# An attention kernel's row maxima: turned on VectorE and spread through DRAM, in place of a turn on TensorE

## The chip, the cores and the metric

The kernel runs on one core of a Trainium2 chip. The metric is the device time of one execution in microseconds (us). Before the change the median of three runs is 1738.05 us (1737.16 to 1738.56). Engines: TensorE (PE; its weight loads are listed as PEld), VectorE (DVE), ScalarE (ACT), GpSimd (POOL) and SyncE (SP), which here only issues transfers.

## The reference

Four layers, A B A B, each a residual branch on x of 2048 tokens by 640 channels, 32 heads of 20 channels, in float32:

```
x = x + A(layernorm(x));  x = x + B(layernorm(x));  x = x + A(layernorm(x));  x = x + B(layernorm(x))

A: linear attention over all tokens, with phi(t) = (t > 0 ? t + 1 : exp(t)) + 1e-6
B: the tokens in 4 segments of 512; in segment s, for each head:
   p     = softmax(q k^T * 20^-0.5 + mask)        # causal inside the segment
   a_dot = p v
   a_mem = phi(q) M / (phi(q) z + 1e-6)           # memory of the segments before s
   o     = sigmoid(beta) * a_mem + (1 - sigmoid(beta)) * a_dot
   M += phi(k)^T v;  z += sum phi(k)
```

The change is in B's softmax. To exponentiate safely, each row of logits (one query of one head) needs its maximum taken off.

## The kernel before, in words

Two streams of work are woven by a small planner in `run` (L1307): `dense` (L1226), which has the projections, layer A, the memories and the output products, and `attend` (L1302), which has the softmax attention of the B layers. Each step yields a cost, and the stream with the lower total goes next; attention yields a fixed `SLOT` after each stretch. PE's instructions keep the order in which the program issues them (`MANUAL`). On the other engines and on SP's queue a list scheduler sets the order: an instruction that it holds ready may go ahead of an earlier one that it holds not ready. `issue_after` puts instructions behind a given one of the same engine.

`attention` (L1104) works on groups of four heads: 8 groups in each of 4 segments in each of 2 B layers, so 64 groups. Each turn of its loop is a **slot** of three **stretches** (L55 to L58), and each entry names an operation and which group it is for: 0 the new one, 1 the one before, 2 the one before that. The dense stream's work comes in between the stretches. So a group goes through three slots:

- `stacks` (L985) loads the group's queries and keys, split into two f16 parts and laid out as 60 rows a head (3 products of 20 channels), from DRAM into `qs` and `ks`: two heads in one half of the partitions (parity 0, rows 0 to 59) and two in the other (parity 1, rows 64 to 123). That is four issues on SP's queue (L993). `qs` and three fixed `ks` rotate, three of each. The entry "load" does this a slot ahead, and puts the issues behind the row transfers issued last (`self.rowed`).
- `row_max` (L998): PE forms the logits of a block of queries against the keys up to it (L1007), and DVE adds the mask and takes the row maximum in one pass (L1013). Five such steps a slot, MAXES 0 to 4, fill `mg`: a 128-partition tile with one value per parity, head and block of 128 queries, 16 columns.
- `split_max` (L1017), at the end of the third stretch: DVE turns the 16 maxima of a query into two f16 parts, negated and scaled (L1022, L1023), in `m2`: 128 x 32.
- `max_rows` (L1027), the entry "rows" in the first stretch of the next slot, after the first group of weighted sums ("sum", 0): PE transposes `m2` with an f16 identity into a PSUM bank (L1031), ACT copies the 32 x 128 result to `mt` (L1033), and two transfers on SP's queue put it into rows 60, 61, 124 and 125 of `qs` (L1036). `ks` holds a constant in the same rows, so the product over 62 rows has the maximum taken off.
- `scores` (L1039): PE's product over 62 rows, keys against queries (L1048), ACT's exp (L1052), POOL's causal mask on the diagonal blocks (L1059). EXPS 0 and 1 come in the second stretch of that same slot, 2 and 3 in the third, 4 at the start of the slot after. EXPS 0 is the first reader of rows 60 and 61 (parity 0), then of 124 and 125 (parity 1).
- `weigh` (L1067) has PE multiply the exponentials with the values, four heads side by side in 32 columns each (L1075), `evacuate` (L1079) copies the sums out (ACT, L1081), and `normalize` (L1083) turns them and divides (L1088 to L1099).

PSUM's eight banks go round for all of this. SP's queue also carries the projections' stores of split queries and keys (`nat` to `qd` and `kd`, L859 to L863), loads of x (L330) and loads of phi(q) (L762, L770). The projections' weights are fetched on POOL's queue (L275).

## Time and profile before

| what | us |
|---|---|
| three runs, median (lowest, highest) | 1738.05 (1737.16, 1738.56) |
| the profiled execution, its own time | 1736.07 |
| its span, first to last instruction | 1734.4 |
| granted TensorE clock, mean | 0.998 of full |
| PE busy | 1666.1 |
| transpose on PE (L1031), 64 times | 14.0 |
| copy on ACT (L1033), 64 times | 16.7 |
| issues of the row transfers (L1036), 128 of 4.0 KB | 0.617 each (median) |

The profile is one execution. "Busy" is the time in which an engine works on an instruction; matmuls are pipelined and overlap, so the sum of their lengths is more than the time that they fill. A group's row gives its line in the kernel, engine, operation, output and inputs by their names, shape and count, then busy time and mean length, then how long the engine stood idle ahead of these instructions and what it waited for (`<-`). In rows of the timeline the first number is the start in us from the span's start, the second the length. A name ending in q (SPq) is an engine's queue of issues: the length of a row there is that of the issue, not of the transfer. The chain of work that ended last is followed back from the last instruction, each step to what released it.

### The profile page before, as it was taken

Reading aid. Unit: us, or ns where it says so; the run is one execution under the profiler, and the core shown is the slowest. Engines: PE = TensorE matmul, PEld = TensorE weight load, DVE = VectorE, ACT = ScalarE, POOL = GpSimd, SP = SyncE. Lnnn points to the kernel's source line nnn. Section 1 sums busy time; section 2 is a strip of 40 time slices with the busy share of each in tenths; the row PEclk is TensorE's granted clock in tenths of the full one; section 3 lists DMA queues with packets and bytes.
Section 4 is the critical chain, followed back from the end, with each engine's and each line's share of the span. In section 5 each row is a group of like instructions: output and inputs, shape, how many; then the busy total and the mean of one; then the engine's idle time right before and its main releaser. Section 6 shows DMA issues by size and latency. Waiting matters only on the chain.

```text
span 1734.4 us, 36014 instructions
## 1 busy us (share of the span) xinstructions
PE 1666.1 (96%) x13032; PEld 1047.5 (60%) x13032; DVE 1180.9 (68%) x3849; ACT 969.7 (56%) x1818; POOL 517.7 (30%) x982
## 2 busy tenths in 40 slices
PE   6999999999999999999999999999999999999998
PEld 4676667664565576556556777666546545645555
DVE  8645534577787677759864456746777877878773
ACT  5545433357557645667675544333665576666673
POOL 1543350012123312334351301221422432233452
PEclk9999999999999999999999999999999999999999
DMA  7522452422322322352211303423232323223432
GB/s 262 184 109 95 150 195 97 139 76 82 113 71 73 113 96 68 120 179 95 78 48 51 103 32 122 175 98 116 75 102 85 112 81 108 93 82 111 131 115 92
DMA packets 118330, 187.58 MB, mean 108 GB/s; under 512 B 13949, under 2 KB 79613, under 8 KB 115849
## 3 DMA queue, kind: packets, MB, share of 16 engines
q1 hardware_dynamic: 105896, 142.68, 25.5%
q0 software_dynamic: 3040, 21.63, 3.4%
q10 hardware_dynamic: 9216, 20.98, 3.1%
q8 instruction: 103, 1.69, 0.4%
q14 instruction: 75, 0.61, 0.1%
HBM read 106.05 MB, written 78.64 MB: 106 GB/s over the span
## 4 chain that ended last, share of the span: by engine, by line
PE 78%; DVE 10%; ACT 6%; issue 2%; POOL 2%; DMA 1%; SPq 1%; ACTq 0%; POOLq 0%; DVEq 0%
PE ps L395 32%; PE ps L381 17%; PE ps L1075 7%; PE ps L1048 4%; ACT pe L1052 3%; PE ps L1007 3%; PE ps L319 3%; PE ps L564 3%; PE ps L450 3%; DVE ps L1013 2%; PE ps L1088 1%; PE ps L891 1%; PE ps L730 1%; DVE st L338 1%; DVE xn L479 1%
## 5 line engine op out<-in xcount | busy, mean ns | idle before, releaser
L1013 DVE CUSTOM_DVE_ANT_0 ps<-ps,maskw 128x512 f32<-128x512 f32 (+3 forms) x1024 | 472.5, 519 | 38.0 <-PE ps L1007 35.7
L1052 ACT ACTIVATE pe<-ps,lsc 128x512 f32<-128x512 f32 x640 | 394.8, 696 | 87.6 <-PE ps L1048 84.9
L1059 POOL TENSOR_SCALAR_AFFINE_SELECT pe<-pe 128x256 f32<-128x256 f32 (+1 forms) x640 | 229.7, 365 | 449.2 <-ACT pe L1052 444.0
L395 PEld LDWEIGHTS <-xT 128*128 128x128 f16 x2880 | 280.3, 98 | 114.6 <-issue 9.3
L395 PEld LDWEIGHTS <-oT 128*128 128x128 f16 x1920 | 185.7, 98 | 80.5 <-issue 7.0
L1075 PE MATMUL ps<-pe,v 128*32 128x512 f32 (+3 forms) x2048 | 162.2, 436 | 11.5 <-POOL pe L1059 5.1
L395 PE MATMUL ps<-w_Bo,oT 128*128 128x320 f16 x960 | 142.3, 302 | 2.8 <-ACT pe L1052 1.1
L1013 DVE DVE_READ_ACCUMULATOR2_ANT mg<- 128x1 f32 x1024 | 143.9, 141 | 0.0
L381 PE MATMUL ps<-xT,w_Bq 128*128 128x512 f16 x600 | 140.2, 380 | 1.9 <-ACT pe L1052 0.8
L395 PE MATMUL ps<-w_Bv,xT 128*128 128x320 f16 x960 | 139.7, 300 | 0.8 <-DVE otok L1095 0.6
L381 PE MATMUL ps<-xT,w_Bk 128*128 128x512 f16 x600 | 138.8, 380 | 1.2 <-ACT pe L1052 1.2
L395 PE MATMUL ps<-w_Ak,xT 128*128 128x320 f16 x960 | 136.1, 300 | 0.0
L1007 PE MATMUL ps<-ks,qs 60*128 60x512 f16 (+3 forms) x1024 | 123.1, 298 | 6.7 <-ACT pe L1052 2.9
L856 DVE SCALAR_TENSOR_TENSOR nat<-ps,nat 128x512 f16<-128x512 f32 x80 | 55.2, 690 | 89.2 <-ACT nat L855 89.1
L1048 PE MATMUL ps<-qs,ks 62*128 62x512 f16 (+3 forms) x1024 | 105.9, 301 | 3.0 <-DMA qs<-mt 1.5
L1075 PEld LDWEIGHTS ps<-pe,v 128*32 128x32 f32 x2048 | 65.3, 109 | 71.9 <-issue 45.8
L421 POOL TENSOR_SCALAR e<-e 128x320 f32<-128x320 f32 (+1 forms) x52 | 82.9, 1594 | 82.4 <-ACT e L417 78.2
L855 ACT ACTIVATE nat<-ps 128x512 f16<-128x512 f32 x80 | 48.2, 603 | 91.8 <-PE ps L381 69.2
L381 PEld LDWEIGHTS <-w_Bk 128*128 128x128 f16 x600 | 57.3, 98 | 65.5 <-issue 5.6
L381 PEld LDWEIGHTS <-w_Bq 128*128 128x128 f16 x600 | 56.7, 98 | 65.9 <-issue 7.8
L1007 PEld LDWEIGHTS <-qs 60*128 60x128 f16 x1024 | 50.0, 94 | 70.9 <-issue 44.7
L343 POOL TENSOR_TENSOR rs<-rs,mhalf 128x1 f32<-128x1 f32 x48 | 27.0, 563 | 218.8 <-DVE rs L342 218.7
(217 smaller groups left out, 2630.7 us busy)
## 6 DMA issues: line engine op xcount, KB each, us to landing
x<-xn ACTq DMA_DIRECT2D x48, 320.0 KB
qs<-qd SPq DMA_DIRECT2D x128, 120.0 KB
ks<-kd SPq DMA_DIRECT2D x128, 120.0 KB
xo<-x SPq DMA_DIRECT2D x48, 320.0 KB
pqi<-pqd SPq DMA_DIRECT2D x32, 320.0 KB
qd<-nat SPq DMA_DIRECT2D x40, 256.0 KB
kd<-nat SPq DMA_DIRECT2D x40, 256.0 KB
x<-in_A_x SPq DMA_DIRECT2D x16, 320.0 KB
```

What stands on the lines that cost most here:

```text
L319: nc.tensor.transpose(pt[:, (c - c0) * P:(c - c0 + 1) * P], src[:, c * P:(c + 1) * P], self.ident)
L381: nc.tensor.matmul(p, w[:, c, a, t * P:(t + 1) * P], xT[:, c, b, :], start=k == 0, stop=k == 3 * C - 1)
L395: nc.tensor.matmul(p, xT[:, c, a, i * P:(i + 1) * P], w[:, c, b, n * HN:(n + 1) * HN], start=k == 0, stop=k == 3 * C - 1)
L421: nc.gpsimd.tensor_scalar(e, e, 1.0, eps, op0=OP.min, op1=OP.add)
L450: nc.tensor.matmul(nd[:, lo - k * cut:hi - k * cut], pq[t], mem[:, OFF[t] + lo - a:OFF[t] + hi - a], start=first, stop=True, skip_group_ch ...
L856: nc.vector.scalar_tensor_tensor(nat[:, 1], p, QK_SHIFT, nat[:, 0], op0=OP.mult, op1=OP.subtract)
L1007: nc.tensor.matmul(bs[par][:, a:a + n], qs[r, p, i * P:(i + 1) * P], ks[r, p, :n], start=True, stop=True)
L1013: nc.vector.tensor_tensor_reduce(bs[par][:, a:a + n], bs[par][:, a:a + n], self.maskw[:, SEG - n:], 1.0, NEG, OP.add, OP.max, G["mg"][:, p ...
L1048: nc.tensor.matmul(b[:, a:a + n], ks[r, p, j * P:(j + 1) * P], qs[r, p, j * P:], start=True, stop=True)
L1052: nc.scalar.activation(e, b, AF.Exp, scale=self.lsc)
L1059: nc.gpsimd.affine_select(d, d, pattern=pat, compare_op=OP.is_ge, fill=0.0, base=0, channel_multiplier=-1)
L1075: nc.tensor.matmul(G["pv"][32 * h4:32 * h4 + 32, j * P:], v[j][:, h * E1:h * E1 + 32], G.pop((p, par, j)), start=j == 0, stop=j == 2, skip ...
```

## The change

The transpose of the maxima goes to DVE, which turns 32x32 blocks each for itself, directly behind the split. The 128 x 32 tile has four such blocks, so that a block holds 32 queries of all 32 columns, in 32 partitions. The tile then goes to DRAM in one transfer (128 pieces of 64 B), and two transfers read it from there into the rows of `qs`, one a parity, in an order of four indices (64 pieces of 64 B each). They read what the first wrote, so SP issues them when it has landed. `max_rows` is gone, with the PSUM bank, the ACT copy and the f16 identity; the transfers are issued at the end of the third stretch of the group's own slot and no longer in the first stretch of the next. "load" moves from the end of the third stretch to the end of the second, so that it stays behind the row transfers of the group before (`self.rowed`), and ahead of those of its own slot.

```diff
-STRETCHES = [[("exp", 4, 2), ("max", 0, 0), ("max", 1, 0), ("sum", 0, 2), ("rows", 0, 1), ("sum", 1, 2), ("sum", 3, 2),
+STRETCHES = [[("exp", 4, 2), ("max", 0, 0), ("max", 1, 0), ("sum", 0, 2), ("sum", 1, 2), ("sum", 3, 2),
               ("sum", 2, 2), ("copy", 0, 2), ("max", 2, 0)],
-             [("out", 0, 2), ("exp", 0, 1), ("exp", 1, 1), ("max", 3, 0)],
-             [("exp", 2, 1), ("exp", 3, 1), ("max", 4, 0), ("split", 0, 0), ("load", 0, 0)]]
+             [("out", 0, 2), ("exp", 0, 1), ("exp", 1, 1), ("max", 3, 0), ("load", 0, 0)],
+             [("exp", 2, 1), ("exp", 3, 1), ("max", 4, 0), ("split", 0, 0)]]
...
-        self.ident16 = cp.tile([P, P], F16, name="ident16")
-        nc.vector.tensor_copy(self.ident16, self.ident)
...
-        G["m2"] = m2
-
-    def max_rows(self, G):
-
-        nc, bp, qs, m2 = self.nc, self.bp, G["qs"], G.pop("m2")
-        pt = self.ps.tile([P, 1024], F16, tag="ps", name="pm", bufs=8)
-        nc.tensor.transpose(pt[:32, :P], m2.rearrange("q a k r -> q (a k r)"), self.ident16)
-        mt = bp.tile([32, P], F16, tag="mt", name="mt", bufs=2)
-        nc.scalar.activation(mt, pt[:32, :P], AF.Copy)
+        mt = bp.tile([P, 32], F16, tag="mt", name="mt", bufs=2)
+        nc.vector.transpose(mt, m2.rearrange("q a k r -> q (a k r)"))
+        md = self.dr.tile([P, 32], F16, tag="md", name="md", bufs=2)
+        self.q_row.dma_start(md, mt)
+        src = md.rearrange("(b a k r) t -> a k r b t", b=NT, a=2, k=2)
         for par in range(2):
             r = 64 * par + 60
-            self.rowed = self.q_row.dma_start(qs[r:r + 2].rearrange("k p (i t) -> k (p i) t", t=P),
-                                              mt[16 * par:16 * par + 16])
+            self.rowed = self.q_row.dma_start(G["qs"][r:r + 2].rearrange("k p (i b t) -> k (p i) b t", b=NT, t=32),
+                                              src[par])
...
-                    elif op == "rows":
-                        self.max_rows(G)
```

## The prediction

> **What bounds the kernel now.** I read the page first: busy shares and the chain that ended last, then the table by stage, then PE's waits.

> ```profile
> PE 1666.1 (96%) x13032; PEld 1047.5 (60%) x13032; DVE 1180.9 (68%) x3849; ACT 969.7 (56%) x1818; POOL 517.7 (30%) x982
> PE 78%; DVE 10%; ACT 6%; issue 2%; POOL 2%; DMA 1%; SPq 1%; ACTq 0%; POOLq 0%; DVEq 0%
> 460.00:920.00 460.00, 445.32 (x3744) 274.95 (x3744) 344.82 (x1244) 289.57 (x541) 149.28 (x326) 1.00 0.29 94
> ```

> TensorE (PE) is the bound: 96% of the span, 78% of the chain. In the longest attention stage (last row: start, end and length, then busy us of PE, weight loads, DVE, ACT, POOL, the clock and the DMA share) PE is busy for 445.32 of 460 us at the full clock. So only PE's own work, or what makes PE wait, moves the time. In the list of PE's waits one row is a row transfer's:

> ```profile
> PE ps L1048 <- DMA qs<-mt: 1.5, 1, 1.5
> ```

> Columns: total us, times, longest. PE waited for the row transfers in one of 64 slots. The question is thus double: what the transpose takes from PE, and whether the new route still delivers its rows before PE asks for them.

> **The change part by part.** *The transpose leaves PE (L1031).*

> ```profile
> L1031 PE MATMUL pm<-ident,m 128*32 128x128 f16 x64 | 14.0, 219 | 2.7 <-DVE m L1023 1.5 <-DVE oT L324 1.2
> 1394.50 1.07 PE L1075 MATMUL ps<-pe,v 128*32 128x512 f32 x8
> 1395.38 0.22 PE L1031 MATMUL pm<-ident,m 128*32 128x128 f16 x1
> 1395.39 1.50 PE L1075 MATMUL ps<-pe,v 128*32 128x384 f32 x24
> L1048 PE MATMUL ps<-qs,ks 62*128 62x512 f16 x256 | 39.0, 382 | 1.5 <-DMA qs<-mt 1.5
> L1048 PE MATMUL ps<-qs,ks 62*128 62x128 f16 x256 | 29.1, 216 | 0.0
> ```

> It shows 64 x 0.219 = 14.0 us, but the next group (L1075) starts 0.01 us after it. Both use 32 of the 128 output columns (128*32): the transpose holds one quarter of the array, the other three go on. What it holds up is its own streaming time. The two L1048 rows give the price of a column: (382 - 216) / (512 - 128) = 0.43 ns, so 128 columns cost 0.055 us. I take 64 x 0.055 = 3.5 us; the bounds are 0.6 us (64 x 0.01) and 14.0 us. [...]

> The first row also has PE's waits ahead of it, 2.7 us, both for DVE. What is late next is DVE itself, which then frees the banks of the next maxima later too. I count half: 1.4 us (bounds 0 and 2.7).

> *The ScalarE copy leaves ACT (L1033).*

> ```profile
> L1033 ACT ACTIVATE mt<-pm 32x128 f16<-32x128 f16 x64 | 16.7, 261 | 16.6 <-PE pm L1031 15.3 <-POOL pe L1059 1.4
>   POOL pe L1059: 1.9, 3
>   PEld ps L319: 0.9, 1
> ```

> The first row: 16.7 us busy and 16.6 us of idling ahead, 33 us of ACT. The other two are who waited for it: 2.8 us. ACT is idle for 44% of the span and PE works beside it, so I count the 0.9 us that reached PE's weight load. At most it is the 2.8.

> *DVE gains 64 block transposes of 128x32 f16.* The trace has none. The nearest rows are the two steps of the split, half as wide:

> ```profile
> L1022 DVE TENSOR_SCALAR m<-mg 128x16 f16<-128x16 f32 x64 | 16.6, 260 | 1.3
> L1023 DVE SCALAR_TENSOR_TENSOR m<-mg,m x64: 124/174/853, 355.8 to 1693.7; 128x16 f16<-128x16 f32 x64
> ```

> Bounds 0.12 and 0.30 us each; I take 0.20, so 12.8 us of DVE time. DVE is idle for a quarter of the attention stages (344.82 of 460), which hides most of it; without that cover it is 12.8 us. I charge 0.2 us to PE.

> *The rows go out earlier, but in two hops.* Before, they start after PE and ACT have had their turn in the next slot. Now they start right behind the split: SyncE (SP) issues mt to DRAM, waits for it to land, then issues the two reads. The room is the stretch from the end of L1023 to the first exp matmul (L1048, 62x512) of the next slot: the first slot, the tightest, the last.

> ```profile
> 355.76 0.12 DVE L1023 SCALAR_TENSOR_TENSOR m<-mg,m 128x16 f16<-128x16 f32 x1
> 365.02 0.61 PE L1048 MATMUL ps<-qs,ks 62*128 62x512 f16 x4
> 1228.16 0.16 DVE L1023 SCALAR_TENSOR_TENSOR m<-mg,m 128x16 f16<-128x16 f32 x1
> 1233.11 0.61 PE L1048 MATMUL ps<-qs,ks 62*128 62x512 f16 x4
> 1693.65 0.17 DVE L1023 SCALAR_TENSOR_TENSOR m<-mg,m 128x16 f16<-128x16 f32 x1
> 1699.12 0.61 PE L1048 MATMUL ps<-qs,ks 62*128 62x512 f16 x4
> ```

> 9.1, 4.8 and 5.3 us. Read so for all 64 slots, less the 0.05 us that PE comes sooner, the rows would be late by 0.3 us in all if the route takes 5.0 us, by 3.2 us at 5.5 (9 slots), 10 at 6.0 (19), 21 at 6.5 (25), 36 at 7.0 (38) and 78 at 8.0 (45). The route's own time comes from these rows:

> ```profile
> 299.10 0.38 SPq L859 DMA_DIRECT2D qd<-nat  x1
> 301.65 0.35 SPq L993 DMA_DIRECT2D qs<-qd  x1
> 309.73 0.34 SPq L862 DMA_DIRECT2D kd<-nat  x1
> 311.84 0.34 SPq L993 DMA_DIRECT2D ks<-kd  x1
> GB/s 262 184 109 95 150 195 97 139 76 82 113 71 73 113 96 68 120 179 95 78 48 51 103 32 122 175 98 116 75 102 85 112 81 108 93 82 111 131 115 92
> 1558.85 1.29 SPq L1036 DMA_DIRECT2D qs<-mt  x2
> 1561.55 0.61 PE L1048 MATMUL ps<-qs,ks 62*128 62x512 f16 x4
> L849 SPq DMA_DIRECT2D ks<-one x6: 563/576/823, 216.8 to 220.0; - x6
> L1036 SPq DMA_DIRECT2D qs<-mt x128: 610/617/699, 359.5 to 1695.8; - x128
> L762 SPq DMA_DIRECT2D pqi<-pqd x16: 518/573/1487, 221.0 to 633.3; - x16
> L859 SPq DMA_DIRECT2D qd<-nat x40: 370/371/1659, 299.1 to 1582.8; - x40
> ```

> First hop: a store of 256 KB that the next load had to wait for took 2.55 and 2.11 us from its issue to the load's. At the 262 GB/s of the busiest slice 256 KB are 1.0 us; ours is 8 KB. So 1.1 to 2.55 us; I take 1.6. Second hop: at 1558.85 the pair issued in 1.29 us and the exp matmul began 1.41 us after it without waiting for it, so the second transfer of a pair lands within 0.62 + 1.41 = 2.03 us of its issue. The new ones carry 64 pieces of 64 B where the old carry 16 of 256 B. From 1 piece a partition (L849, 0.576) to 8 (L1036, 0.617), both into two partitions, the issue grows by 0.006 us a piece: 24 more make 0.14 us. From L859 (2 pieces, 0.371) to L762 (5, 0.573) it is 0.067: 1.6 us. I take 0.14, since those rows have the same two partitions, and 0.25 us more for reading from DRAM. Sum: 0.20 transpose + 0.10 hand-over + 1.6 + (0.62 + 0.14 + 0.06) for the first read's issue + (2.03 + 0.14 + 0.25) = 5.1 us. The low end is about 4.0 (0.12 for the transpose, 1.1 for the first hop, no surcharges), the high end about 9 (0.30, 2.55, 1.6 more for each issue). At 5.1 the rows are late by 0.8 us in all; for traffic and other issues in SP's way I put it at 2.2 us.

> One slot shows the traffic: the row transfers took 5.26 us behind a 1.6 MB weight fetch on POOL's queue. This wait (the 1.5 us above) stays, as both hops fall into the same fetch.

> ```profile
> 701.20 0.60 POOL L275 DMA_DIRECT2D w_Ak<-wd_Ak  x1 [0.27 <-PE ps L395]
> 703.13 5.26 DMA qs<-mt
> SPq L1036 <- ACT mt L1033: 435.3, 61, 21.1
> ```

> *SP's queue.* SP stood 435.3 us before L1036 with all else queued behind. It now stands before the store for DVE instead, and some 1.6 us more before the reads; behind it are the nat stores, xo and pqi loads and the next stacks. Against that it no longer waits for PE and ACT, so what is behind it moves by little: nothing charged, at most 1.6 us in a slot where a nat store holds PE. *The stacks* (four L993 issues a slot) still follow the previous group's row transfers and come a stretch sooner in the program; they have most of a slot until their first use. Nothing charged; if that cover went, PE would wait for them as it does in no row of its list now. The dropped f16 identity is one copy in the opening: nothing.

> Sum: -3.5 - 1.4 - 0.9 + 0.2 + 2.2 = -3.4 us. The profiled execution took 1736.07 us (span 1734.4), 1.98 below the median of the three runs, 1738.05; against its own time that is 1732.7, against the median 1734.6.

> **The rivals.** *Rows late (slower).* PE stalls at the first exp matmul of a slot as soon as the route takes over 4.8 to 5.0 us. For it: the nearest slots have no room left, everything goes to two partitions in 64 B pieces, and there are two hops to be caught in traffic. Against it: the row pair alone lands within 2.03 us. At 6.5 us it costs 21 us: -5.6 + 21 = +15, 1753 us; at 6.0, +4.6, 1743. [...]

> *Swallowed (no change).* PE comes 0.05 us earlier in each slot and waits as much longer for masks or banks: 1738. For it: PE already idles 3% of these stages. Against: no single wait stands there to take it up.

> *The transpose was serial (faster).* Were all 0.22 us paid, -14 in place of -3.5: 1724. The 0.01 us speaks against it. [...]

> *It does not do what it says.* SP's order is set by a planner. In one slot three loads held SP for 5.39 us, then three more ahead of the row transfers:

> ```profile
> 577.20 5.39 SPq L993 DMA_DIRECT2D ks<-kd  x3
> 582.70 0.81 SPq L993 DMA_DIRECT2D qs<-qd  x2
> 583.57 0.41 SPq L993 DMA_DIRECT2D ks<-kd  x1
> 584.68 1.28 SPq L1036 DMA_DIRECT2D qs<-mt  x2
> ```

> If such loads come ahead of the store, the rows start no earlier and yet make two hops: 2.0 us late (582.70 to 584.68) in every sixth slot is some 10 x 2.0 = 20, less 5.6: 1752.

> **How the numbers follow.** Forecast, a small gain of 1.5 to 8 us: 0.45. Swallowed: 0.17. Rows late: 0.26. Serial transpose: 0.05. Not as said: 0.07. A measurement of this kernel tells about 0.2% (3.5 us) from no change: the forecast's own middle lies on that line, so I split it 0.40 faster and 0.05 the same. Faster: 0.40 + 0.05 = 0.45; same: 0.05 + 0.17 = 0.22; slower: 0.26 + 0.07 = 0.33. The forecast's own range is 1730 to 1737. The range given is 1728 to 1752: below it are most of the serial case (0.04) and a gain of over 10 us from ACT (0.02), above it a route of over 6.4 us (0.10) and the worse half of the last case (0.03).

> **What would show it.** Right: no L1031 and L1033, some 0.2 us for the DVE transpose, the first read issued about 1.7 us after the store, and PE's waits for qs at L1048 staying within 3 us. Wrong: an idle row of PE at L1048 put down to the row transfers over 10 us; reads issued over 0.8 us each; L1075 starting far sooner than 0.05 us against before; or new waits of ACT for nat (L855), which would mean that SP's longer stand holds the stores.

## The result, and the profile after

The changed kernel is slower: 1755.4 us median of four runs (1751.24 to 1756.78) against 1738.3 us (1737.16 to 1739.73), a ratio of 1.0094 with a 95% interval of 1.0075 to 1.0113. That is 17 us more, where a gain of 3.4 was forecast. The profiled execution has a span of 1753.5 us, 19.1 more than that of before.

First the page's engine row and the chain of the kernel after.

```profile
PE 1670.2 (95%) x12968; PEld 1045.3 (60%) x12968; DVE 1189.2 (68%) x3912; ACT 957.5 (55%) x1754; POOL 519.0 (30%) x982
...
PE 73%; DVE 11%; ACT 6%; DMA 5%; issue 3%; POOL 2%; SPq 1%; ACTq 0%; POOLq 0%; DVEq 0%
```

PE is as busy as it was (1666.1 before), so its idle time went from 68 to 83 us. The chain has given 5% to DMA, which had 1%. Next the list of waits of the kernel after: engine, line, what it waited for; total us, times, longest.

```profile
SPq L1026 <- DVE mt L1024: 295.9, 44, 18.5
SPq L1030 <- DMA md<-mt: 70.7, 54, 7.5
...
ACT nat L853 <- DMA kd<-nat: 6.5, 1, 6.5
PE ps L1069 <- DVE rc L458: 6.0, 1, 6.0
PE ps L1042 <- DMA qs<-md: 5.7, 4, 5.0
PE ps L317 <- DMA ol<-od: 3.3, 2, 1.9
```

L1026 is the store of the turned maxima, L1030 the two reads, L1042 the exp matmul (L1048 before), L1069 the weighted sums (L1075 before), L853 the nat copy (L855 before), L860 the store of nat to kd that holds it (L862 before), L273 the weight fetch (L275 before). PE waits for the rows 5.7 us in all, and 5.0 of them are one slot. So it is not that all slots are a little late.

To see where the time is lost, I laid PE's instructions of the two traces side by side, one by one, and followed the difference of their starts. By the times of the kernel before, it stays under 2.2 us up to 680 us, jumps by 5.1 at 708 us and by 8.4 around 782 us, and grows by another 6 between 1345 us and the end, in steps of mostly 0.5 to 1.6. **Two places make 13.5 of the 19.1 us.** The first, in the chain of waits around it (start, length, what) and in POOL's timeline:

```profile
702.05 0.60 POOL L273 DMA_DIRECT2D w_Ak<-wd_Ak  x1 [0.27 <-PE ps L393]
```

```profile
702.39 0.22 DVE mt L1024
702.62 0.02 issue
702.63 7.83 DMA md<-mt
...
710.53 2.13 DMA qs<-md
712.66 0.04 issue
712.70 1.49 PE ps L1042 x4
```

A weight fetch of 1.6 MB goes out at 702.05. The 8 KB store of the maxima, 0.6 us behind it on another engine's queue, takes 7.83 us until SP is released. Only then can the reads start, which add 2.13 us. Before, the one hop fell into the same fetch and took 5.26 us in all.

The trace also records every packet that the DMA engines move (queue, start, length and size; no view lists them). Each of the two transfers ends with 16 packets of 4 B: the fetch's come from 707.67 to 709.08, and the store's from 707.70 to 709.15, each 27 to 69 ns behind one of the fetch's. Of the store's 128 packets of 64 B, 48 move before the first of these, so the two take turns; but the store is through only when the fetch is.

The second place, from the same view of the kernel after:

```profile
782.41 8.14 DMA kd<-nat
...
790.65 0.61 ACT nat L853
791.26 0.02 issue
791.28 0.69 DVE nat L854
791.98 0.09 DVE rc L458
792.07 0.06 issue
792.12 4.50 PE ps L1069 x32
```

A store of nat goes out at 782.41, 0.71 us behind the next fetch (issued at 781.70), and takes 8.14 us. Its buffer is one of two, so ACT can't write the next nat; DVE stands behind ACT, and PE's sums stand for DVE (the 6.0 us above). By the packets, a load of x issued ahead of this store on SP's queue (781.33) takes turns with the fetch from 783.76 on, and the store's own 128 packets move only from 788.98 to 790.11.

Both losses come with a slower clock. The table by stage of the kernel after (start and end, length, then busy us and count of PE, weight loads, DVE, ACT and POOL, then the granted clock, DMA share and GB/s):

```profile
690.00:705.00 15.00, 15.00 (x155) 8.63 (x147) 12.39 (x49) 9.88 (x20) 5.80 (x14) 1.00 0.31 86
712.00:718.00 6.00, 5.30 (x29) 1.94 (x29) 1.64 (x8) 2.51 (x5) 1.17 (x4) 0.72 0.46 138
792.00:798.00 6.00, 5.88 (x38) 2.60 (x39) 4.06 (x18) 3.59 (x6) 6.00 (x6) 0.50 0.47 148
798.00:804.00 6.00, 5.60 (x47) 4.67 (x47) 5.48 (x23) 2.89 (x6) 0.85 (x4) 0.99 0.00 0
```

After the idle of 5.0 us TensorE gets 0.72 of its clock for 6 us, after the 6.0 us it gets 0.50: another 6 x 0.28 = 1.7 and 6 x 0.50 = 3.0 us lost. At the first place 5.0 - 1.5 (the wait of before) + 1.7 = 5.2 us, which is the jump of 5.1. At the second 6.0 + 3.0 = 9.0 us, 0.6 over the jump of 8.4. In the trace the clock is 0.50 from 712.74 to 716.16 us and from 791.25 to 798.08. What sets it off is not shown, and it is not the length of PE's idle alone: in the kernel before, the clock is 0.50 from 1092.8 to 1096.2 us, with PE busy for 1.50 of the 3.40 us ahead of that, and of two shorter idles at the first place in the runs below, one of 2.7 us (one hop) is followed by a clock of 0.50 and one of 3.1 us (changed, both fetches cut) is not.

### The profile page after: what moved, and what is told of

The parts are those of the page before. It is cut to its first block, busy times and chain, and to the rows that moved or that the text cites. A ratio compares the mean times of both kernels' runs of the same rounds, so it can differ in the third digit from the quotient of the medians.

```text
span 1753.5 us, 36006 instructions
## 1 busy us (share of the span) xinstructions
PE 1670.2 (95%) x12968; PEld 1045.3 (60%) x12968; DVE 1189.2 (68%) x3912; ACT 957.5 (55%) x1754; POOL 519.0 (30%) x982
## 4 chain that ended last, share of the span: by engine, by line
PE 73%; DVE 11%; ACT 6%; DMA 5%; issue 3%; POOL 2%; SPq 1%; ACTq 0%; POOLq 0%; DVEq 0%
PE ps L393 30%; PE ps L379 16%; PE ps L1069 7%; ACT pe L1046 3%; PE ps L1042 3%; PE ps L317 3%; PE ps L562 3%; PE ps L1005 3%; PE ps L448 3%; DVE ps L1011 2%; PE ps L889 1%; PE ps L1082 1%; DMA md<-mt 1%; PE ps L728 1%; DVE st L336 1%
## 5 line engine op out<-in xcount | busy, mean ns | idle before, releaser
L1069 PE MATMUL ps<-pe,v 128*32 128x512 f32 (+3 forms) x2048 | 163.2, 441 | 19.8 <-POOL pe L1053 6.9
L1069 PEld LDWEIGHTS ps<-pe,v 128*32 128x32 f32 x2048 | 64.3, 110 | 102.4 <-issue 77.3
L1042 PE MATMUL ps<-qs,ks 62*128 62x384 f16 (+3 forms) x1024 | 107.8, 301 | 6.3 <-DMA qs<-md 5.7
L853 ACT ACTIVATE nat<-ps 128x512 f16<-128x512 f32 x80 | 48.3, 604 | 95.7 <-PE ps L379 72.4
L341 POOL TENSOR_TENSOR rs<-rs,mhalf 128x1 f32<-128x1 f32 x48 | 27.4, 572 | 223.5 <-DVE rs L340 216.8
```

Of the source, the lines that this page charges most:

```text
L1042: nc.tensor.matmul(b[:, a:a + n], ks[r, p, j * P:(j + 1) * P], qs[r, p, j * P:], start=True, stop=True)
L1069: nc.tensor.matmul(G["pv"][32 * h4:32 * h4 + 32, j * P:], v[j][:, h * E1:h * E1 + 32], G.pop((p, par, j)), start=j == 0, stop=j == 2, skip ...
```

## The experiments

Theories. **A**: the loss is in transfers held up, in two forms. A1: SP stands for the store's landing, and what is queued behind it goes late. A2: small transfers fall behind the weight fetches. **B**: the rows go out too late, since they have to wait for the store. **C**: the work taken from PE and ACT was worth nothing. Each ran beside the kernel before on the same chip, in four sets; its median there was 1737.3 to 1738.4 us.

| run | median us | ratio to before (95%) |
|---|---|---|
| changed, both fetches cut | 1746.93 | 1.0046 (1.0032 to 1.0060) |
| before, both fetches cut | 1736.48 | 0.9994 (0.9985 to 1.0002) |
| one hop | 1736.25 | 0.9990 (0.9979 to 1.0001) |
| one hop at the old place | 1735.76 | 0.9988 (0.9979 to 0.9997) |
| reads after the yield | 1759.55 | 1.0113 (1.0096 to 1.0130) |
| one hop, store unread | 1737.11 | 0.9990 (0.9981 to 0.9999) |
| one hop, SP stands beside it | 1736.19 | 0.9989 (0.9981 to 0.9998) |
| the same, both fetches cut | 1736.20 | 0.9993 (0.9985 to 1.0001) |
| changed, first fetch cut | 1744.71 | 1.0043 (1.0030 to 1.0056) |
| changed, second fetch cut | 1749.90 | 1.0076 (1.0063 to 1.0089) |
| rows behind the stand (order undone) | 1737.29 | 1.0001 (0.9991 to 1.0012) |
| rows of the last store | 1740.51 | 1.0017 (0.9998 to 1.0036) |
| rows forced behind the stand | 1753.43 | 1.0091 (1.0066 to 1.0115) |
| the same, both fetches cut | 1749.98 | 1.0070 (1.0057 to 1.0082) |
| changed, exp later | 1762.47 | 1.0147 (1.0129 to 1.0165) |
| before, exp later | 1745.40 | 1.0043 (1.0030 to 1.0057) |

### Cutting the fetches

```diff
-        self.q_w.dma_start(w, self.wd[key])
+        for c in range(C):
+            self.q_w.dma_start(w[:, c], self.wd[key][:, c])
```

> The changed kernel, with each 1.6 MB weight fetch on POOL's queue cut into five of 128 pieces of 2,560 B. Theory A (held transfers): 13.5 of the 17 to 19 us come from two places in which a small transfer stood behind such a fetch (the rows' store 7.8 us, a nat store 8.1 us); if short pieces let it through sooner, 1742 to 1746 us. Theory B (the route of the rows is too long in every slot): no change, 1755. If the five fetches hold other queues as long as the one did, A is not refuted by 1755: then the two waits of 7.8 and 8.1 us are still in the trace.

> The kernel before with the same cut fetches, the control for the run above. Theory A: the one wait of 1.5 us for the rows behind a fetch goes, and little else, 1736 to 1738 us. Theory B: 1738. Four more issues for each fetch cost POOL some 0.6 us each, which it has.

Measured: 1746.9, so 8.5 us come back, a little less than A2 asked for. The kernel before doesn't change by more than a measurement tells (1736.5). Then each fetch alone:

> The changed kernel with only the weight fetch at 702 us cut in five, the one behind which the rows' store stood for 7.8 us. If the second loss (8.4 us at 782, where a store of nat stands behind the next fetch) is a knock-on of the first, both go: 1745 to 1748 us, as with both fetches cut (1746.9). If it is a collision of its own, only the first goes: 1751 to 1754.

> The changed kernel with only the fetch at 782 us cut in five. If the second loss is a knock-on of the first or a collision of its own, the cut takes away what the long fetch itself holds: 1747 to 1750 us with the first loss (5 us) still there. If it is no matter of that fetch, 1755.

Cutting the first alone gives 1744.7: both losses go, as was expected of a knock-on. Cutting the second alone gives 1749.9: the first stays, and of the second PE still waits 2.1 us, where it waited 6.0. Chain and timelines (PE, then POOL) of the kernel with the first cut:

```profile
703.52 3.02 DMA md<-mt
```

```profile
711.22 0.84 PE L1046 MATMUL ps<-qs,ks 62*128 62x512 f16 x4 [2.62 <-DMA qs<-md]
```

```profile
702.94 1.15 POOL L275 DMA_DIRECT2D w_Ak<-wd_Ak  x2 [0.27 <-PE ps L397]
704.81 1.65 POOL L275 DMA_DIRECT2D w_Ak<-wd_Ak  x3
```

The same store now takes 3.02 us, not 7.83, and PE waits 2.62, not 5.00. The fetch's pieces are of 12,800 B, one for each of 128 partitions; cut, they are of 2,560 B. But the store, issued at 703.52, doesn't stand behind all five parts: POOL issues two from 702.94 on and the other three from 704.81 on. By the packets the store ends 60 ns behind the first part, on each of the 16 (705.30 to 705.88, the first part's 705.24 to 705.82). So with the cut the store stands behind a fifth of the bytes; whether shorter pieces would help with all five parts ahead of it is not shown. Nor is why a store ends only with the fetch ahead of it: in the changed kernel each packet of the whole fetch is one piece of 12,800 B, and 48 packets of the store move before the first of the fetch's 4 B packets.

Is the second loss a knock-on of the first? In the traces with the second fetch whole, the question is how far ahead of it the nearest store of kd on SP's queue goes out:

| kernel | store ahead of fetch, us | ACT's wait for kd |
|---|---|---|
| before, one hop (three kinds), rows behind the stand | 1.6 to 2.1 | none |
| one hop, SP stands beside it | 1.8 | none |
| reads after the yield | 1.0 | 6.0 |
| rows of the last store | 0.9 | 5.1 |
| changed, first fetch cut | -0.03 | none |
| rows forced behind the stand | -0.3 | 8.1 |
| changed | -0.7 | 6.5 |

So it is a collision of its own, decided by about one microsecond; the late rows of the first place are one way to move the store to the wrong side. The run with rows of the last store has it without any first loss. The kernel with the first fetch cut seems an exception, but its packets explain it: the second fetch's first packet comes 2.57 us after its issue, at 781.69 (1.32 us in the changed kernel), and of the store's 128 packets, which start from 781.01 to 782.18, 71 have gone by then. So the order of the issues alone doesn't decide. In the run with the reads after the yield the store's packets start 0.45 us ahead of the fetch's and last from 783.00 to 788.85; here they start 0.68 us ahead and go free. Why a fetch starts 1.3 to 2.6 us after its issue stays open.

### One hop

```diff
-        md = self.dr.tile([P, 32], F16, tag="md", name="md", bufs=2)
-        self.q_row.dma_start(md, mt)
-        src = md.rearrange("(b a k r) t -> a k r b t", b=NT, a=2, k=2)
...
-                                              src[par])
+                                              mt[16 * par:16 * par + 16, None].to_broadcast([16, NT, 32]))
```

> The changed kernel without the hop through DRAM: the two reads take the rows straight from the transposed tile, as 64 pieces of 64 B as before. It leaves out the maxima of three of four 32-query blocks and uses those of the first in their place. SP then stands for nothing between the split and the reads. Theory A: the rows' store can't be held (5 us back), and SP is free some 1.5 us sooner in every slot (4 to 6 us back); whether the nat store gets ahead of its fetch again (8 us) hangs on SP's timing: 1738 to 1747 us. Theory B: rows come 1.5 us sooner, all of the loss goes: 1733 to 1737. Theory C (the work taken from PE and ACT was worth nothing and DVE's new work costs): at least 1750.

Measured: 1736.2, below what A gave and within B's. Without the hop nothing of the loss is left.

> The kernel before with only the transpose exchanged: VectorE turns the blocks at the split, and the two row transfers go straight from that tile at their old place and time in the order, the loads too. It leaves out the maxima of three of four 32-query blocks and uses those of the first in their place. It prices what TensorE's transpose and the ScalarE copy were worth. By the prediction's terms 3.5 + 1.4 + 0.9 - 0.2 = 5.6 us: 1732 to 1734 us. Theory C: 1738 or more. With no effect that can be measured: 1737 to 1739.

Measured: 1735.8, 2.1 us below before, between the 1732 to 1734 of the prediction's terms and the 1737 to 1739 of no effect. So C is not the cause of the loss: without the hop the new kernel is no slower than before. What the removal is worth is under the 5.6 expected, and at 2.1 us hardly more than a measurement tells. Split place or old place makes no difference (1736.25 against 1735.76).

### What in the hop costs

The next runs put the hop back piece by piece, behind the one-hop reads. The run with the store unread has only the first two of these lines.

```diff
+        md = self.dr.tile([P, 32], F16, tag="md", name="md", bufs=2)
+        self.q_row.dma_start(md, mt)
+        mu = bp.tile([2, 32], F16, tag="mu", name="mu", bufs=2)
+        self.rowed = self.q_row.dma_start(mu, md[:2])
```

> The one-hop kernel (1736.25) with the store of the turned maxima to DRAM added behind the two reads; nobody reads it and SP waits for nothing. It leaves out the maxima of three of four 32-query blocks and uses those of the first in their place. It prices the added store alone, 64 times 0.32 us of SP and 8 KB each. Theories A and B: the store itself costs nothing, 1735 to 1738. If the transfer itself or its issue is the cost: 1745 or more.

> As the run above, and behind the store a small read of what it wrote, into a tile that nobody uses: SP stands until the store has landed, as in the changed kernel, but the rows went out ahead of it and depend on nothing of it. It leaves out the maxima of three of four 32-query blocks and uses those of the first in their place. Theory A (SP's stand and the transfers queued behind it): most of the 19 us between the one-hop kernel and the changed one come back, 1748 to 1756. Theory B (the rows themselves are late): 1735 to 1739.

> The run above with each weight fetch cut in five. It leaves out the maxima of three of four 32-query blocks and uses those of the first in their place. With the changed kernel (1755.4), the same with cut fetches (1746.9), and the run above it makes four corners: rows behind the hop or beside it, fetches whole or cut. Theory A: what SP's stand alone costs without the long fetches, 1740 to 1747. Theory B: as the one-hop kernel, 1735 to 1738. If this run is below 1739 while the run above is above 1745, the stand costs only where a long fetch holds it.

Measured: 1737.1, 1736.2 and 1736.2. **A1 falls** as the cause of the large losses; a part of it comes back at the kernel's end (below). SP stands in the kernel with the stand beside it as it does in the changed one. SP's waits of the run with the stand beside it, and SP's timeline at the first place:

```profile
SPq L1032 <- DMA md<-mt: 63.8, 48, 5.3
```

```profile
702.09 1.32 SPq L1027 DMA_DIRECT2D qs<-mt  x2
703.46 0.70 SPq L1030 DMA_DIRECT2D md<-mt  x1
709.58 0.25 SPq L1032 DMA_DIRECT2D mu<-md  x1
709.93 0.78 SPq L991 DMA_DIRECT2D qs<-qd  x2
```

63.8 us of standing against 70.7, 5.3 of them in this slot, the stacks issued only at 709.93 (711.91 in the changed kernel), and no loss. What differs is that the rows went out at 702.09. They landed behind the fetch too, but once: chain and timeline of the same kernel.

```profile
702.09 6.12 DMA qs<-mt
```

```profile
708.26 0.83 PE L1043 MATMUL ps<-qs,ks 62*128 62x512 f16 x4 [1.09 <-DMA qs<-mt]
```

PE waits 1.09 us here, 5.00 in the changed kernel. Is it the late start, then, or the reading from DRAM?

> The changed kernel with the store and a small read of it in front, for which SP stands as before, and then the two row reads, but straight from the transposed tile and not from DRAM. It leaves out the maxima of three of four 32-query blocks and uses those of the first in their place. The rows go out when they do in the changed kernel (0.3 us later), on the way of the one-hop kernel. If the lateness of their start is the whole cost: 1752 to 1758 us. If it is the reading from DRAM: 1736 to 1740.

Measured: 1737.3, but the run didn't do what it was made for. The scheduler put the row reads ahead of the small read that waits, so it repeats the run with the stand beside it, and shows no gain over before (1737.34). The order was forced in the next two, whose reads still come straight from the tile:

```diff
+        stood = self.q_row.dma_start(mu, md[:2])
...
+            with self.tc.issue_after(stood.ins):
```

> What the run of rows behind the stand was to be, with the order forced: in that run the planner had put the row reads ahead of the small read that waits, so they did not stand. Here SP issues the store, waits for its landing with the small read, and only then sends the rows straight from the transposed tile. It leaves out the maxima of three of four 32-query blocks and uses those of the first in their place. If the late start of the rows is the whole cost: 1752 to 1758 us, with the loss at 706 us back. If it is the reading from DRAM: 1736 to 1740.

> The run above with both weight fetches cut in five. It leaves out the maxima of three of four 32-query blocks and uses those of the first in their place. If the 9 to 10 us that stay in the changed kernel with cut fetches (1746.9 and 1744.7) are the rows' late start in the other slots, 1744 to 1748. If they come of reading the rows from DRAM: 1736 to 1739.

Measured: 1753.4 with whole fetches, the changed kernel again (1755.4) without one row read from DRAM; 1750.0 with cut ones, 2 us over the range expected. At the first place the chain of the run with whole fetches has the same shape:

```profile
701.80 6.69 DMA md<-mt
708.48 0.02 issue
708.50 0.25 SPq L1028
708.75 0.05 issue
708.81 0.65 SPq L1032
```

So at the first place it is the late start of the rows, B, but not at each slot's expense. At the second the nat store is 0.3 us behind the fetch and ACT waits 8.1 us.

> The changed kernel in which the two reads take the maxima that the group before stored, so from DRAM in 64 pieces of 64 B as in the changed kernel, but SP waits for no store. It leaves out each group's own maxima and uses those of the group before. If the wait for the store, before which the rows can't start, is the whole cost: 1735 to 1739 us. If reading the rows from DRAM costs by itself: 1745 or more.

Measured: 1740.5, with runs from 1732.9 to 1748.9; between the two expectations. In its profiled execution the first place loses nothing, and the second loss is there alone, from its chain:

```profile
773.00 8.27 DMA kd<-nat
```

So reading from DRAM costs nothing at the first place, and the spread would fit a collision that is there in some executions and not in others; with one trace this is not shown.

> The changed kernel with the store of the turned maxima at the split as before, and the two reads as an operation of their own at the start of the next slot in the program, behind the dense work that is woven in between. SP's order then lets loads and stores of the dense stream go between store and reads. Theory A1 (SP stands for the landing, and what is queued behind it comes late): part of the loss comes back, 1746 to 1752 us, and SP's wait ahead of the reads falls below 40 us in all (70.7 now). Theory B (rows late): the reads come later still, 1757 to 1770, and PE's waits for qs at the exp matmuls rise above 10 us in all.

Measured: 1759.6, in B's range, but without the sign of either theory: PE waits 4.2 us in all for the rows (5.7 in the changed kernel), and SP still stands 69.2 us ahead of the reads. At the first place no other transfer goes between store and reads. So the run doesn't tell A1 from B; it has the second loss (ACT waits 6.0 us for kd) and a profiled clock of 0.989.

### More room for the rows

> The changed kernel with the maxima of the third part ahead of the first two exp blocks in each slot's second stretch, so that PE asks for the rows some 0.3 to 0.5 us later (four 384-wide or 256-wide matmuls). If small lateness in many slots makes the rest of the loss, some of it comes back: 1748 to 1753 us; if the loss sits in the two collisions with fetches alone, 1754 to 1757.

> The kernel before with the same exchange of the maxima and the exp blocks, the control for the run above. Its rows are late in one slot by 1.5 us only: 1736 to 1740 us. What it gains or loses is the exchange's own price.

Measured: 1762.5 and 1745.4, both above every range expected. The exchange costs 7 to 8 us in both kernels, so these runs say nothing about the rows.

### What stays when both fetches are cut

10.7 and 13.8 us against the run with the rows ahead (1746.9 and 1750.0 against 1736.2). In the trace of the changed kernel with both cut I find four parts, measured against the run with cut fetches and the stand beside the rows. The first place still loses 2.1 us and the second 1.3. Three slots lose 0.6 to 0.7 each, two of them in this way (timeline of this kernel, then of the run with the stand beside):

```profile
1346.98 2.36 PE L1071 MATMUL ps<-pe,v 128*32 128x512 f32 x32 [0.49 <-ACT pe L1048]
```

```profile
1344.10 2.36 PE L1072 MATMUL ps<-pe,v 128*32 128x512 f32 x32
```

In the compiled program the first sum of these two slots waits for ACT's exp, where in the other kernel it waits for DVE and an earlier matmul: banks and waits are laid out anew. That the planner does so because it reckons with a later row is argued and not shown. The same two steps are in the run with forced order. Last, the end region, where loads of ol stand on SP's queue behind store, wait, reads and stacks: 2 us. Chain of the changed kernel:

```profile
1643.04 2.73 DMA md<-mt
...
1649.03 4.25 DMA ol<-od
1653.28 0.14 issue
1653.42 0.53 PE ps L317 x3
```

That is 7 us of the 6.5 by which the two traces differ at the end (other places gain a little). The other 4 us of the medians go with the clock: over six runs of this kernel the span falls from 1748.6 us at a mean clock of 0.991 to 1740.8 at 0.997, and the profiled one has 0.997. In every kept trace the clock halves for 3.41 us or a multiple of it (from 712.74 to 716.16 and from 791.25 to 798.08 in the changed kernel), and one such stretch is 0.001 of the mean (half of 3.41 us in some 1750). The profiled executions have from 2 to 11 of them within the span; why one execution gets more than another stays open.

## Why the prediction was wrong, point by point

- **DVE's transposes**: forecast 0.20 us each, hidden. Right, by the group's row of the kernel after, and by the one-hop runs, which have them and are no slower than before.

```profile
L1024 DVE STREAM_TRANSPOSE mt<-m 128x32 f16<-128x32 f16 x64 | 13.2, 206 | 1.6
```

- **What PE and ACT save**: -3.5 - 1.4 - 0.9 + 0.2 = -5.6 us forecast. The five one-hop runs gain 1.3 to 2.2, the run of rows behind the stand, which repeats one of them, 0.05. The mis-sized term is the transpose. Laid side by side, PE starts the sums behind it a median 0.009 us sooner without it: 64 x 0.009 = 0.6 us, the low bound, which was the row's own 0.01 us. I had taken the streaming time of 128 columns, 0.055 us, in its place. The trace of before agrees with a transpose that holds a quarter of the array: of the four matmuls that follow it, three start 0.008, 0.014 and 0.021 us after it and the fourth 0.056 (medians of 64). With 0.6 for it the sum is -2.7, so the other two gains may be too large as well; no run parts them. The timeline of after shows the 32 sums of that slot in one piece of 2.36 us; before, from 1394.50 to 1396.89, they took 2.39 with the transpose in their middle.

```profile
1408.77 2.36 PE L1069 MATMUL ps<-pe,v 128*32 128x512 f32 x32
```

- **The route**: forecast 5.1 us from the split's end to the rows' landing. The median of 64 is 4.9 and the least 4.3. The first read goes out 1.47 us after the store (median; least 1.41), where 1.7 was forecast, and the second lands 2.05 us after its issue. The issues cost what they did before, so the surcharge of 0.14 us was not needed:

```profile
L1030 SPq DMA_DIRECT2D qs<-md x128: 593/621/710, 359.7 to 1715.3; - x128
```

- **Late rows in general**: 2.2 us forecast; PE's waits at L1042 outside the one slot are 0.7. Right, and the rival "rows late", 10 to 21 us spread over the slots, is not what happened.
- **The slot of the weight fetch. This step failed**: "This wait (the 1.5 us above) stays, as both hops fall into the same fetch." They don't. The second hop can't be issued before the first has landed, and the first lands when the fetch is through (the store's last packets 27 to 69 ns behind the fetch's); what was a wait beside the fetch became the fetch plus a hop. 1.5 us of waiting became 5.0, and 1.7 more went with the clock.
- **SP's queue and the nat stores. This step failed too**: "nothing charged, at most 1.6 us in a slot where a nat store holds PE." That SP's stand costs no more than a measurement tells when the rows go out ahead of it is shown (1736.2). But the price of a nat store gone late isn't how late it is: it is the fetch that it falls behind, 8.1 us, and 8.4 us for PE. The prediction named this sign, "new waits of ACT for nat (L855)", and gave it no chance and no price beyond the 1.6. It also read the sign as a store held by SP's longer stand; no transfer of the maxima is issued on SP's queue between 768.1 and 791 us, so here it is the fetch.
- **Swallowed, serial transpose, not as said**: none of the three. The time, 1755.4, lies beyond the range's upper end of 1752, since its top came from lateness spread over slots and not from two collisions. The rival "rows late" has the right direction and names "two hops to be caught in traffic", but it prices only the room in each slot.

The place of the loss and its size at whole fetches are shown by cutting the fetches and by the forced order. Left open are what moves the nat store against the second fetch, why a fetch starts early or late after its issue, and what sets the clock from run to run. No version beats both kernels by more than a measurement tells: the one-hop runs gain 0.1%, and they leave out three quarters of the maxima. A one-hop version with all of them, with a read for each block, was not tried.

## What to carry to other kernels

A transfer that waits for another has to be priced at the worst traffic that its first half can meet, not at its quiet time: here the two halves shared no queueing delay, the 2.13 us of the read came on top of the store's 7.83. So list the large fetches with their times, and for each ask which transfers that PE will wait for now go out from a microsecond ahead of it until it is through, or have to be repeated behind it. And a long idle of TensorE can be paid again in clock: here those of 5.0 and 6.0 us were (0.72 and 0.50 of the clock for the next 6 us), of two around 3 us one was.
